# A strided convolution with its gradients on one Trainium2 core: branch A of the first batch split one level further, and the second batch's output gradient turned inside its gelu stage

## The chip, the core and the metric

The program runs on one core of one Trainium2 chip. The metric is the device time of one execution, in microseconds (us); the kernel before took 1272.7 us, the median of 3 runs (1272.4 to 1275.49). The core has a matrix engine (TensorE, PE in the profile; its weight loads are PEld), a vector engine (VectorE, DVE), a scalar engine (ScalarE, ACT), GpSimd (POOL) and SyncE (SP). Each works through its own list of instructions in order and waits for the others by semaphores. Transfers between DRAM and the on-chip memory (SBUF) are issued here mostly from SP, the transposing ones always, and from POOL; 16 DMA engines carry them out. The accumulators of TensorE (PSUM) are eight banks, used here as four tiles of two banks each.

## The reference, cut to what matters

```python
B, T, D, K = 2, 16000, 256, 31      # x is (B, T, D), w is (K, D, D), bf16
s = 2
L = (T - K) // s + 1                # 7985
h = sum over i < K of x[:, i:i + s*L:s, :] @ w[i]      # strided convolution
mu  = sum over l of h / L;  var = sum over l of (h - mu)**2 / L     # per batch and channel
y = gelu((h - mu) / sqrt(var + 1e-5) * gn_gamma + gn_beta)          # tanh form
returns y and, for a given grad_out, the gradients for x, w, gn_gamma, gn_beta
```

The heavy parts are three convolutions of one size: the forward one, the one that gives the gradient of x, and the one that gives the gradient of w.

## The kernel before

**Stages.** In order of time: the forward convolution of batch 0 (four chunks of 512 column pairs, `c` = 0 to 3), the forward convolution of batch 1 with the gelu of batch 0 (its value, its slope and the gradient through it) beside it, the gradient of x for batch 0 with the gelu of batch 1 beside it, the gradient of x for batch 1, and the gradient of w. TensorE's own work never stops for a stage of the others: gelu, normalization and turning of layouts are put beside matmuls on DVE, ACT, POOL and the DMA queues.

**The branches.** The convolution is computed by a splitting of the taps into three products in place of four, applied at two levels. At the first level the taps fall into the branches A, B_ and C_; the inputs of a branch are sums of neighbouring input parts (`sums`) and its weights are parts or differences of the weights (`w_diff`, `w_mid`). Inside each branch the same is done again: its leaves A (`mk_la`) and C_ (`mk_lc`) and its middle product, whose inputs are `mk_ux` and whose weights are `W[br][:, B_]`. The middle product is always computed at a third level (`l3_first` with the weights `WX`, then `l3_rest`). A branch in `self.deep` has its two leaves split a third time as well: `mk_deep` makes two more sums on DVE (tiles `lh` and half of `l`), the leaf needs `rest`, 32 matmuls, and 16 more of a shared product (`third` with the weights `WD`), instead of 64 matmuls. All have 128 x 128 weights and 256 columns (230 or 231 in parts of the last chunk).

In the kernel before `self.deep` holds C_ alone in chunk 0 of batch 0, B_ and C_ in chunks 1 to 3, and nothing in batch 1.

**The order of a chunk.** `fwd_chunk_fixed` writes out the steps in `STEPS`: F (first part of the middle product), L0 and L1 (the leaves), R (rest of the middle product). Two steps, L0 and L1 of "prev", finish branch C_ of the chunk before. `RING` gives each branch two of the four PSUM tiles, `px` and `pt`: the middle product is made in `px`, copied with changed signs to `pt` (`l3_neg`, `seed`, or an ACT copy), and the leaves are accumulated onto it. After each step the functions listed by the number of the step put DVE's work for the steps to come into its list. All this is fixed in program order, so that an instruction that waits holds up everything behind it on its engine.

**The clock of the plan.** Side work is placed by a clock that is counted up with every step (`side_work`, which is `advance`) by an assumed duration, 1.75 for an F step, 3.5 for R, 7.0 for an L step (times .75 where the branch is split). `at(t, fn)` emits `fn` at the first step that ends at or after t. `PLAN` holds such times: loads and parts of the second set of weights (`w2`), turning of the output gradient (`got`, `late`), the gelus (`g0`, `g1`), the elementwise gradient (`e`).

**The second set of weights.** The gradient of x needs the weights with rows and columns turned. `w2_load` turns them with four DMA transposes into a tile `vr` (one buffer, tag "in"), `w2_comp` takes two differences into a tile `vd` on DVE and stores six pieces to DRAM (`vl`), from where they are loaded after the forward stage.

**The output gradient.** The gelu needs grad_out with channels on the partitions. `got_turn` makes that by one DMA transpose for each of eight units (`gt` tiles). For batch 0 this is done in its gelu stage and `grad` works on the `gt` tile. For batch 1 it is done early, beside the forward stage of batch 0: `got_store` writes it to DRAM (`got_d`), and `gelu_load` fetches it again (`gg` tiles) in the gelu of batch 1.

Where the profile names L125, the instruction went through the small recording class `Engine`; L160, L162 and L170 are `w_mid` and `w_deep`. The groups are told apart by the names of tiles: `la`, `lc`, `lh` are leaf inputs, `lx` is `ux`, `s` the sums, `wx` and `wd` the third-level weights, `hs` the evacuated result, `junk` the squares for the statistics, `rb` branch B_'s results.

## Time and profile before

| what | value |
|---|---|
| median of 3 runs | 1272.7 us (1272.4 to 1275.49) |
| the profiled execution | 1270.96 us, of which the span from first to last instruction is 1269.1 us |
| granted TensorE clock, mean | 0.999 |
| busy share of PE, DVE, ACT, POOL | 97%, 71%, 40%, 22% |
| matmuls | 7692 |
| DMA traffic | 252.73 MB, mean 199 GB/s |
| HBM read and written | 136.42 MB, 68.63 MB |

The profile was taken on one execution, which was 1.7 us faster than the median of the others. A page of the profile gives busy time by engine, the span in 40 slices, the DMA queues, the chain of work that ended last, and the costliest groups of instructions. Beside it the trace can be asked for the instructions of a stretch in order of time (start, duration, engine, operation, tiles, and in brackets the idle time before it with what ended it), for groups by shape, for waits, and for the busy time of each engine in given stretches. Durations of merged matmuls include the end of the last one's pipeline; the distance from one start to the next is what a group takes of TensorE's time.

### The profile page before, as it was taken

To read this page: it belongs to the slowest core of one execution; us is meant where nothing else is said; L and a number is where in the kernel's file an instruction comes from. 1 tells how busy PE (TensorE), PEld (TensorE's weight loads), DVE (VectorE), ACT (ScalarE), POOL (GpSimd) and SP (SyncE) were. 2 spreads that over 40 slices of the span, in tenths; PEclk is the share of its full clock that TensorE was granted. 3 is DMA by queue.
4 is the path that set the end of the run, shared out by engine and by line. 5 is a ranking of instruction groups with operands and counts; after the bars stand their busy time and mean duration, and the time that the engine had idled before them with its cause. 6 is when DMAs were issued, how large, how long until landed. Compare 5 with 4: busy or idle time off the path is not lost.

```text
span 1269.1 us, 19006 instructions
## 1 busy us (share of the span) xinstructions
PE 1233.0 (97%) x7692; PEld 758.6 (60%) x7692; DVE 901.7 (71%) x1080; ACT 504.0 (40%) x679; POOL 279.8 (22%) x410
## 2 busy tenths in 40 slices
PE   4899999999999999999999999999999999999998
PEld 2788889988888964444445444445444444444444
DVE  3967656578988687989876596685576755876482
ACT  0032423489888568989853333222011010101000
POOL 2013201112222433445333331100000000110043
PEclk9999999999999999999999999999999999999999
DMA  9979987439997796998649995455894795997895
GB/s 199 176 153 196 215 150 138 79 77 197 185 164 159 208 305 157 208 226 234 172 148 107 241 237 121 127 183 170 277 325 150 232 333 188 322 337 262 252 226 127
DMA packets 289335, 252.73 MB, mean 199 GB/s; under 512 B 197128, under 2 KB 260616, under 8 KB 284128
## 3 DMA queue, kind: packets, MB, share of 16 engines
q1 hardware_dynamic: 254448, 152.60, 50.7%
q0 software_dynamic: 30576, 96.82, 29.7%
q10 hardware_dynamic: 4224, 2.10, 0.8%
q8 instruction: 60, 0.98, 0.3%
q14 instruction: 27, 0.22, 0.1%
HBM read 136.42 MB, written 68.63 MB: 162 GB/s over the span
## 4 chain that ended last, share of the span: by engine, by line
PE 49%; DVE 3%; issue 2%; DMA 1%; ACT 1%; POOL 1%; POOLq 0%; DVEq 0%; ACTq 0%
PE wps L125 28%; PE ps L125 20%; DVE D L125 1%; DMA dyd<-gg 1%; DMA x<-in_x_dram 1%; DVE ps L125 0%; DVE et L125 0%; DVE le L125 0%; DVE go L125 0%; DVE ux L125 0%; POOL he L125 0%; DVE s L125 0%; DMA gg<-got 0%; DVE vk L125 0%; ACT gy L125 0%
## 5 line engine op out<-in xcount | busy, mean ns | idle before, releaser
L125 PEld LDWEIGHTS <-w 128*128 128x128 bf16 x3360 | 327.5, 98 | 57.7 <-issue 10.5
L125 PE MATMUL ps<-v,le 128*128 128x512 bf16 (+3 forms) x1152 | 259.2, 375 | 2.6 <-DVE ps L125 2.4
L125 PEld LDWEIGHTS <-le 128*128 128x128 bf16 (+1 forms) x1280 | 129.9, 102 | 144.8 <-issue 4.3
L125 PEld LDWEIGHTS <-x 128*128 128x128 bf16 x1248 | 122.0, 98 | 144.6 <-DVE x L125 0.6
L125 PE MATMUL ps<-la,w 128*128 128x256 bf16 (+2 forms) x1200 | 135.2, 273 | 18.0 <-DVE la L125 17.7
L125 PE MATMUL wps<-dl,x 128*128 128x512 bf16 (+1 forms) x704 | 150.8, 374 | 0.0
L125 ACT ACTIVATE ps<-ps 128x1024 f32<-128x1024 f32 (+3 forms) x115 | 85.2, 741 | 147.0 <-PE ps L125 147.0
L125 PE MATMUL ps<-lc,w 128*128 128x256 bf16 (+2 forms) x1168 | 129.2, 270 | 0.0
L125 ACT COPY p<-wps 128x1024 f32<-128x1024 f32 x28 | 28.4, 1013 | 211.2 <-PE wps L125 106.7
L125 DVE TENSOR_TENSOR go<-ps,rg 128x1024 bf16<-128x1024 f32 (+1 forms) x64 | 78.0, 1220 | 43.8 <-PE ps L125 29.1
L125 POOL DMA_DIRECT2D out_dram<-we x31 | 22.5, 726 | 334.6 <-DVE we L125 334.6
L125 PE MATMUL ps<-v,ux 128*128 128x512 bf16 (+1 forms) x384 | 90.7, 379 | 3.6 <-DVE ux L125 1.9
L125 PE MATMUL wps<-dl,xe 128*128 128x512 bf16 x416 | 91.7, 379 | 0.0
L125 PE MATMUL ps<-lx,w 128*128 128x256 bf16 (+2 forms) x768 | 86.9, 270 | 1.8 <-ACT ps L125 1.3
L125 ACT ACTIVATE gy<-gh,stats 128x1024 bf16<-128x1024 bf16 x64 | 76.6, 1228 | 7.3 <-DMA gh<-hd 7.3
L125 PE MATMUL wps<-D,x 128*128 128x512 bf16 x352 | 77.1, 379 | 0.0
L125 PEld LDWEIGHTS <-xe 128*128 128x128 bf16 x416 | 40.7, 98 | 49.1
L125 PEld LDWEIGHTS <-ux 128*128 128x128 bf16 (+1 forms) x384 | 38.7, 101 | 49.3 <-DVE ux L125 3.6
L125 ACT ACTIVATE hs<-ps 128x512 bf16<-128x512 f32 (+1 forms) x64 | 36.7, 578 | 75.9 <-PE ps L125 75.9
L125 DVE TENSOR_TENSOR ps<-ps,rb 128x1024 f32<-128x1024 f32 (+1 forms) x37 | 38.0, 1028 | 36.2 <-ACT rb L125 28.3
L125 ACT COPY rg<-ps 128x1024 f32<-128x1024 f32 (+1 forms) x32 | 32.2, 1007 | 69.2 <-PE ps L125 67.4
L125 DVE SCALAR_TENSOR_TENSOR gz<-gy,gy 128x1024 bf16<-128x1024 bf16 x32 | 39.1, 1222 | 23.9 <-ACT gy L125 22.8
(170 smaller groups left out, 1708.4 us busy)
## 6 DMA issues: line engine op xcount, KB each, us to landing
x<-in_x_dram SPq DMA_DIRECT2D x29, 1024.0 KB, 8.6
xe<-in_x_dram SPq DMA_DIRECT2D x20, 1024.0 KB, 9.2
S<-dnd SPq DMA_DIRECT2D x16, 1216.0 KB, 8.3
D<-dnd SPq DMA_DIRECT2D x12, 1216.0 KB, 9.2
out_dram<-go POOLq DMA_DIRECT2D x28, 512.0 KB, 4.2
gh<-hd POOLq DMA_DIRECT2D x32, 256.0 KB, 7.3
dnd<-dn POOLq DMA_DIRECT2D x32, 256.0 KB, 4.4
E<-dnd SPq DMA_DIRECT2D x6, 1216.0 KB, 10.6
```

Of the source, the lines that this page charges most:

```text
L125: ins = fn(*a, **k)
```

## The change

Three things are changed together.

1. In chunks 1 to 3 of batch 0 branch A is split like B_ and C_. Its shared third-level products come in two new steps, V and T, and F accumulates onto V in the same PSUM tile: V (leaf A's product into `px[A]`), an ACT copy of it to SBUF (`l3_keep`), L0 of B_, F, T (leaf C_'s product into `pt[A]`), a DVE sum (`l3_sum`), R, and then two DVE operations that make `pt[A]` (`l3_seed`) in place of an ACT copy. `w_deep(A)` makes the weights. The lists of DVE work by step are rearranged, also for batch 1, and the clock counts a split leaf with half of 7.0 instead of three quarters.
2. The output gradient of batch 1 is turned inside the gelu of batch 1, as for batch 0. The stores to `got_d`, the loads from it and the tiles `gg` are gone.
3. `w2_comp` takes the differences in place in `vr` instead of in `vd`; the stores of the unchanged parts come earlier, in `w2_keep`. Some times of the plan are moved: the `w2` parts, the first elementwise part of the gradient stage, the statistics of batch 1, and the places of `w2x_comp(A)` and of `mk_l(B_)` at the start of the gradient stage. `small` has one buffer instead of two, `wd` six instead of four.

```diff
-            t = WD[br, lf] = side["p"].tile([P, 2, 2, 2, D], BF16, name="wd", tag="wd", bufs=4)
+            t = WD[br, lf] = side["p"].tile([P, 2, 2, 2, D], BF16, name="wd", tag="wd", bufs=6)
...
+    def w2_keep(q, raw):
         sl = slice(q * 512, (q + 1) * 512)
-        for br, r1 in ((A, 0), (C_, 1)):
+        for br, r1 in ((C_, 1), (A, 0)):
             for slot, r2 in ((A, 0), (C_, 1)):
                 gq.dma_start(out=vl_d[br][:, slot // 2, :, sl], in_=raw[:, :, r2, r1, :])
+    def w2_comp(q, raw):
+        sl = slice(q * 512, (q + 1) * 512)
+        for slot, r in ((A, 0), (C_, 1)):
+            ve.tensor_tensor(out=raw[:, :, r, 1, :], in0=raw[:, :, r, 1, :], in1=raw[:, :, r, 0, :], op=ALU.subtract)
+            gq.dma_start(out=vl_d[B_][:, slot // 2, :, sl], in_=raw[:, :, r, 1, :])
...
-            self.deep = () if b else (C_,) if c == 0 else (B_, C_)
+            self.deep = () if b else (C_,) if c == 0 else ORDER
...
+        def l3_leaf(self, br, lf, ps):
+            l = self.l[br, lf]
+            self.third(ps[:, 0], (l[0] if isinstance(l, tuple) else l)[:, 1], WD[br, lf])
+        def l3_keep(self, px):
+            self.v = side["m"].tile([P, 512], FP32, name="vf", tag="jk", bufs=1)
+            ac.copy(out=self.v[:], in_=px[:, 0, :])
+        def l3_sum(self, pt):
+            ve.tensor_tensor(out=self.v[:], in0=pt[:, 0], in1=self.v[:], op=ALU.add)
+        def l3_seed(self, px, pt):
+            ve.tensor_tensor(out=pt[:, 0], in0=self.v[:], in1=px[:, 0], op=ALU.subtract)
+            ve.scalar_tensor_tensor(out=pt[:, 1], in0=px[:, 1], scalar=-1.0, in1=self.v[:], op0=ALU.mult, op1=ALU.subtract)
...
-                at(clock[0] + 2, lambda: self.squares(br))
+                at(clock[0] + 1.5, lambda: self.squares(br))
...
+        if A in k.deep:
+            steps[4:7] = [(4, "V", A, 1.75), (5, "L0", B_, 7.0), (12, "F", A, 1.75), (13, "T", A, 1.75), (6, "R", A, 3.5)]
...
-            side_work(us * (.75 if own and what[0] == "L" else 1))
+            side_work(us * (.5 if own and what[0] == "L" else 1))
...
-            for fn in {0: (lambda: k.sums(A),), 1: (lambda: k.mk_lc(B_),), 2: (lambda: k.mk_la(A),), 3: (lambda: k.mk_ux(A),),
-                       5: (lambda: k.mk_lc(A), lambda: k.sums(C_)), 6: (lambda: k.mk_la(C_),),
+            for lf in {1: (A,), 4: (C_,)}.get(n, ()):
+                if B_ in k.deep:
+                    k.mk_deep(B_, lf)
+            for fn in {0: (lambda: k.sums(A),), 1: (lambda: k.mk_lc(B_), lambda: k.mk_la(A)), 3: (lambda: k.mk_ux(A),),
+                       4: (lambda: k.mk_lc(A),),
+                       5: (lambda: k.sums(C_),), 6: (lambda: k.mk_la(C_),),
...
-            for br, lf in {1: ((B_, A),), 4: ((B_, C_),), 8: ((C_, A),), 9: ((C_, C_),)}.get(n, ()):
+            for br, lf in {6: ((A, A),), 8: ((A, C_),), 9: ((C_, A),)}.get(n, ()):
...
-    def got_store(c, e, gt):
-        for dh in range(2):
-            gq.dma_start(out=got_d[c][e][:, dh], in_=got_view(c, gt, dh))
...
-        go = new("gg", 1)
-        gq.dma_start(out=go[:], in_=got_d[c][e][:, dh])
-        return h[:], go[:]
+        return h[:]
...
         def turn_in(u):
-            if b == 0 and u < 8:
-                gts[u] = got_turn(0, *units[u])
+            if u < 8:
+                gts[u] = got_turn(b, *units[u])
...
-    PLAN = dict(got=(22, 42, 64, 84, 120), late=(2, 11), w2=((3, 16), (29, 43), (52, 66)),
+    PLAN = dict(w2=(6, 14, 48, 82),
...
-                e=((0, 1, None, None, 3, 5.5), (0, 2, 30, 38, 56, 63), (0, 3, 92, 98, 114, 121), (1, 0, 172, 180, 203, 208),
+                e=((0, 1, None, None, 9, 13), (0, 2, 30, 38, 56, 63), (0, 3, 92, 98, 114, 121), (1, 0, 172, 180, 203, 208),
...
+    at(7, lambda: w_deep(A))
...
+    at(PLAN["w2"][0], lambda: w2_comp(0, wr.pop(0)))
+    for q, t in zip((1, 2, 3), PLAN["w2"][1:]):
+        at(t, lambda q=q: wr.__setitem__(q, w2_load(q)))
+        at(t + 13, lambda q=q: w2_keep(q, wr[q]))
+        at(t + 25, lambda q=q: w2_comp(q, wr.pop(q)))
...
-    at(1.8, lambda: fwd_stats(1))
+    at(4.5, lambda: fwd_stats(1))
...
     kn.mk_ux(B_)
-    kn.mk_l(B_)
     kn.sums(A)
     w2x_comp(C_)
+    kn.mk_l(B_)
...
-            marks[0][A, "R"] = [lambda: w2x_comp(A)]
+            marks[0][A, "R"] = marks[0][A, "L0"]
+            marks[0][A, "L0"] = [lambda: w2x_comp(A)]
```

More of the change, by code (lines that the diff above doesn't have):

```diff
@@ L518, in fwd_chunk_fixed @@
                 k.l3_neg(px[br])
+            elif what == "V":
+                k.l3_keep(px[A])
+            elif what == "T":
+                k.l3_sum(pt[A])
+            elif what == "R" and br == A:
+                if deep:
+                    k.l3_seed(px[A], pt[A])
+                else:
+                    ac.activation(out=pt[A][:], in_=px[A][:], func=ACT.Copy, scale=-1.0)
+                ve.tensor_tensor(out=px[A][:], in0=px[A][:], in1=rb[:, 0], op=ALU.add)
             elif what == "R" and (br == C_ or own):
@@ L1454, in conv_stem_kernel @@
     epool = tc.tile_pool(name="ep", bufs=1, side="right", reuse_waits="tile")
-    for i, t in zip((6, 7), PLAN["late"]):
-        parked(i, t)
     done = gelu_plan(0, *PLAN["g0"])
```

65 lines of the change are left out of this document (26 added, 39 removed).

## The prediction

> **What bounds the kernel now.** The page comes first: its busy times say which engine has no room.
>
> ```profile
> PE 1233.0 (97%) x7692; PEld 758.6 (60%) x7692; DVE 901.7 (71%) x1080; ACT 504.0 (40%) x679; POOL 279.8 (22%) x410
> ```
>
> TensorE is busy for 1233.0 of 1269.1 us, but an average over stages does not say where a saved matmul shortens the run. So the second view is the busy time by stretch, for chunks 1, 2 and 3 of batch 0's forward stage and for the start of the gradient stage (columns: stretch, length, busy PE, PEld, DVE, ACT, POOL with counts, granted clock, DMA share, GB/s).
>
> ```profile
> 77.90:129.20 51.30, 51.30 (x466) 45.13 (x465) 38.45 (x50) 17.30 (x33) 12.72 (x17) 1.00 0.85 167
> 129.20:180.50 51.30, 51.30 (x467) 45.10 (x466) 32.23 (x43) 17.30 (x33) 9.93 (x13) 1.00 1.11 206
> 180.50:228.60 48.10, 48.10 (x467) 45.14 (x465) 30.82 (x44) 17.21 (x33) 4.66 (x7) 1.00 0.60 111
> 459.60:480.20 20.60, 17.41 (x79) 7.27 (x78) 18.88 (x33) 17.31 (x24) 3.84 (x6) 1.00 0.83 238
> ```
>
> In the three chunks that the change touches TensorE has no idle time at all, at full clock, while DVE is busy for 30.82 to 38.45 us of some 50. There a removed matmul is removed time, as long as DVE and ACT, in their fixed order, still come before it. The last row is the opposite: 20.60 - 17.41 = 3.2 us of idle TensorE where the gradient stage begins, with DVE at 18.88. The change moves DVE work there too.
>
> **Part 1, the matmuls removed.** The third view is TensorE's list in order of time; a group's cost is the distance to the next start. First an unsplit leaf and a split one of full width:
>
> ```profile
> 106.31 1.92 PE L125 MATMUL ps<-s,wx 128*128 128x256 bf16 x16
> 108.07 7.18 PE L125 MATMUL ps<-la,w 128*128 128x256 bf16 x64
> 115.09 3.71 PE L125 MATMUL ps<-lx,w 128*128 128x256 bf16 x32
> ...
> 154.04 1.94 PE L125 MATMUL ps<-lc,w 128*128 128x256 bf16 x16
> ...
> 157.60 1.92 PE L125 MATMUL ps<-s,wx 128*128 128x256 bf16 x16
> ...
> 169.93 1.94 PE L125 MATMUL ps<-la,wd 128*128 128x256 bf16 x16
> 171.70 1.94 PE L125 MATMUL ps<-lc,wd 128*128 128x256 bf16 x16
> ```
>
> Branch A's leaf takes 115.09 - 108.07 = 7.02 us. A split leaf takes 157.60 - 154.04 = 3.56 us for its 32 matmuls, and its shared product 171.70 - 169.93 = 1.77 us. Split, a leaf is 7.02 - 3.56 - 1.77 = 1.69 us shorter; chunks 1 and 2 have four such leaves: 6.76 us. In chunk 3 only the 230 or 231 wide parts shrink:
>
> ```profile
> 204.20 1.75 PE L125 MATMUL ps<-lc,w 128*128 128x231 bf16 x16
> ...
> 207.37 1.92 PE L125 MATMUL ps<-s,wx 128*128 128x256 bf16 x16
> 209.13 6.51 PE L125 MATMUL ps<-la,w 128*128 128x231 bf16 x64
> 215.48 3.34 PE L125 MATMUL ps<-lx,w 128*128 128x231 bf16 x32
> 218.66 1.94 PE L125 MATMUL ps<-la,wd 128*128 128x256 bf16 x16
> 220.44 1.94 PE L125 MATMUL ps<-lc,wd 128*128 128x256 bf16 x16
> ```
>
> (215.48 - 209.13) - (207.37 - 204.20) - (220.44 - 218.66) = 6.35 - 3.17 - 1.78 = 1.40 us, twice 2.80. Together **9.56 us** less of TensorE, with 96 fewer matmuls (32 a chunk).
>
> **Part 2, what the split asks of DVE and ACT.** Their rows, by shape, over the three chunks (mean ns):
>
> ```profile
> L125 DVE TENSOR_TENSOR ps<-ps,rb 128x1024 f32<-128x1024 f32 x9 | 11.1, 1230 | 7.9 <-ACT ps L125 4.7 <-ACT rb L125 3.2
> L125 DVE TENSOR_TENSOR ps<-ps,rb 128x512 f32<-128x512 f32 x12 | 8.4, 700 | 23.1 <-ACT rb L125 22.9
> L125 DVE TENSOR_TENSOR la<-s,s 128x2064 bf16<-128x2064 bf16 x6 | 7.4, 1225 | 0.0
> L125 DVE TENSOR_TENSOR lh<-la 128x1028 bf16<-128x1028 bf16 x6 | 4.2, 697 | 5.3 <-PE ps L125 5.3
> L125 ACT ACTIVATE hs<-ps 128x512 bf16<-128x512 f32 x22 | 12.9, 593 | 40.4 <-PE ps L125 40.4
> L125 ACT ACTIVATE junk<-hs 128x1024 bf16<-128x1024 bf16 x12 | 12.6, 1053 | 0.2
> L125 ACT ACTIVATE ps<-ps 128x512 f32<-128x512 f32 x9 | 5.2, 582 | 5.7 <-PE ps L125 5.7
> ```
>
> Each chunk gains four leaf sums of 0.70, one `l3_sum` and two `l3_seed` operations of 0.70 on DVE: 4.9 us, on 38.45 at most, in a chunk that shrinks to 51.3 - 3.4 = 47.9 us. That is 90%, so it is a question of order, not of load. With the starts of TensorE's groups laid out anew from F of branch B_ (0 us), R of A ends at 28.35, L1 of B_ at 31.9, F of C_ at 33.7, and L0 of A follows. Between R and L0, 3.56 + 1.76 = 5.32 us, DVE must do the two seeds, the 128x1024 addition to `px[A]`, `mk_la(C_)` and both halves of `mk_deep(A, A)`: 1.40 + 1.23 + 1.23 + 1.40 = 5.26 by the rows. This is the tightest place: about 0.1 us late in chunks 1 and 2, and in chunk 3, where L1 is 3.17, the window is 4.93 and the list 0.3 to 0.4 late. I charge **+0.5 us**; the bounds are 0 (successive starts lie up to 0.1 apart less than the durations) and 3 (0.2 us of handing over on each of five operations, in three chunks).
>
> The ACT copy between V and F has cover: after L1 of "prev" ACT does two evacuations, two squares and the copy, 1.2 + 2.1 + 0.6 = 3.9 us, while TensorE does V and L0 of B_, 1.77 + 3.56 = 5.3 us. Without these 1.4 us F would wait. Branch C_'s seeds now have L1 of A (3.56) and F (1.76) to hide in instead of 7.02 + 1.76: the ACT copy after the leaves (1.0) and two additions (1.4) end 2.4 us after the leaves, 2.9 us in time. `w_deep(A)` (two operations of 1.2 us) stands where DVE waited for ACT's `rb` before (22.9 us in that row) and costs nothing.
>
> **Part 3, the second weights in place.** DVE's subtraction now overwrites data whose stores must have landed, and the next load must wait for the stores of the difference. Rows for the loads, the wait for them, and the landing of the stores (KB each, median us from issue):
>
> ```profile
> 96.72 14.09 SPq L125 DMA_TRANSPOSE vr<-in_w_dram  x4
> ...
> 115.99 0.69 DVE L125 TENSOR_TENSOR vd<-vr 128x1024 bf16<-128x1024 bf16 x1 [1.59 <-DMA vr<-in_w_dram]
> ...
> vl<-vr POOLq DMA_DIRECT2D x16, 256.0 KB, 6.2
> ```
>
> The four loads of one part took up to 115.99 - 96.72 = 19 us. In the new order part 1 can be loaded from some 18 us into chunk 1 (the difference of part 0 at 11.6, then its stores), is there at 30 to 37, and its stores land 7 us later, at 37 to 44; DVE comes to the subtraction at 40, just ahead of branch C_'s seeds, which have 2.5 us to spare. Part 2 is loaded from about 1 us into chunk 2, stored by 20 to 27, and wanted at 25.6, where DVE would idle until R of A ends at 28.35. Part 3 has more room. So each waits between nothing and 1.5 us beyond its cover; I take **+0.6 us** in sum, with bounds 0 and 3. The load on the DMA engines falls here, which is why I take the lower half: seven of the eight units of grad_out and their stores leave these chunks.
>
> **Part 4, grad_out turned in the gelu.** What a turned byte costs the DMA engines is read from two stretches: 129.2 to 180.5, where q1 carries only transposes, and 893 to 1139, where it carries plain loads (columns: packets, MB, share of 16 engines); the third row is POOL's queue from 480.2 to 660, the last the median us to landing of a unit of grad_out in the first stretch.
>
> ```profile
> q1 hardware_dynamic: 24635, 6.20, 80.2%
> ...
> q1 hardware_dynamic: 45232, 65.41, 79.3%
> ...
> q0 software_dynamic: 9735, 31.88, 64.6%
> ...
> gt<-in_grad_out_dram SPq DMA_TRANSPOSE x4, 7.2
> ```
>
> Transposes: 0.802 x 51.3 / 6.20 = 6.6 us of all engines for a MB; plain loads 0.793 x 246 / 65.41 = 3.0; POOL's transfers 0.646 x 179.8 / 31.88 = 3.6. Eight turned units of 0.52 MB take 27 us of the gelu stage's 180 and sixteen `gg` loads of 0.26 MB give 15 back: the mean share there rises by 12 / 180 = 0.07. [...]
>
> It adds no time, because each unit is asked for two halves of the gelu (22 us) before `grad` needs it and lands in 7.2. SP's list takes eight more instructions among the dn transposes, which are only stored for a later stage; POOL's loses 32. DVE's and ACT's operations keep their shapes. I charge **0**, bounds -0.5 and +1.
>
> **Part 5, the start of the gradient stage.** TensorE's idle there is in these waits:
>
> ```profile
> 459.62 1.02 PE L125 MATMUL ps<-vx,et 128*128 128x512 bf16 x4
> ...
> 461.53 1.89 PE L125 MATMUL ps<-v,ux 128*128 128x512 bf16 x8 [0.89 <-ACT ps L125]
> ...
> 468.78 1.89 PE L125 MATMUL ps<-v,ux 128*128 128x512 bf16 x8 [0.48 <-ACT ps L125]
> ...
> 475.21 1.04 PE L125 MATMUL ps<-vx,s 128*128 128x512 bf16 x4 [1.10 <-DVE vx L125]
> ...
> 480.18 1.90 PE L125 MATMUL ps<-v,ux 128*128 128x512 bf16 x8 [0.48 <-DVE ux L125]
> ```
>
> `w2x_comp(A)` moves ahead of the elementwise part and of `mk_l(C_)`, 2.8 us of DVE, and the second sign copy ahead of ACT's square root; that takes away most of 1.10 + 0.48 + 0.48. Against it, batch 0's last gelu halves are emitted later: the clock now counts 3.5 us less in front of them, so their last product stands behind R of A of the last chunk instead of before it, and with it the elementwise part that ends in `vx`, the first weights of the stage.
>
> ```profile
> 444.62 0.76 DVE L125 TENSOR_SCALAR et<-et,stats 128x2080 bf16<-128x2080 bf16 x1 [5.29 <-DMA et<-dyd]
> ...
> 455.68 1.22 DVE L125 TENSOR_TENSOR vx<-v 128x2048 bf16<-128x2048 bf16 x1
> ```
>
> By the order of the lists that product now has the addition and `mk_la(C_)` ahead of it, 2.46 us by part 2's rows; its store and the loads `et` follow. I take 1.8, since they took DVE's time before, too. `vx` was done 459.62 - 456.90 = 2.7 us ahead of its use, so the delay shows only in the waits of `vx` for C_ and of `le`, some 1 us in all. Net **-1.0 us**, bounds -2.2 (all three waits gone, no delay) and +3.5 (the 3.5 us of clock in full, nothing gained). The 177 us of batch 1's forward stage have slack of one leaf step at each hand-over; the shuffle of DVE's list there is put at **+0.4**, bounds 0 and +2.
>
> **The sum.** -9.56 + 0.5 + 0.6 + 0 - 1.0 + 0.4 = -9.1 us on the profiled execution of 1270.96: 1261.9. That execution was 1.7 us below the median of the runs shown, so the median to expect is 1272.7 - 9.1 = **1263.6 us**.
>
> **Rivals.** They are priced from the forecast. A wait of TensorE can cost more than itself: after one of 2.33 us 16 matmuls took 3.01 us, where the row at 106.31 has 1.92, so 1.1 us more.
>
> ```profile
> 53.36 3.01 PE L125 MATMUL ps<-s,wx 128*128 128x256 bf16 x16 [2.33 <-DVE wx L162]
> ```
>
> [...]
>
> - *The list between R and L0 sets the pace.* If each chunk loses 1 to 1.5 us there and the weights' waits come to 2 us, the gain halves: 1263.6 + 2.5 to 3.5 + 1.4 = about 1268. For it speaks the 5.26 us in a window of 5.32; against it DVE's successive starts, which lie closer than its durations.
> - *The gelu ends too late for the gradient stage.* Part 5 comes out at +3.5 instead of -1.0: 1268.1. For it speaks that the elementwise part already waited 5.29 us for its load; against it the 2.7 us between `vx` and its use.
> - *More is gained.* All waits of part 5 go and the emptier DMA queues keep DVE from waiting at all: 1272.7 - 9.56 - 2.2 = 1260.9.
> - *Slower than before.* The in-place subtraction of part 2 in chunk 2 holds DVE. With loads of 19 us and stores of 10 us (an estimate, above the row's 6.2) part 1's stores land at 18 + 19 + 1 + 10 = 48 us instead of by 42.5: 5.5 lost. Its difference is stored at 60, 12 us into chunk 2; part 2's stores land there at 12 + 19 + 1 + 10 = 42, where the cover ends at 28.35: 13.6 lost. With twice 1.1 that is 21 us: 1285. It decides from 9.1 us lost in these two places. What speaks against it is a DMA share that falls in these chunks.
>
> **How the numbers follow.** The forecast (1260.5 to 1266) has 0.60, the two rivals near 1268 together 0.22, the greater gain 0.07, the slower one 0.06, and 0.05 is left for a result near no change by several of these together. A measurement of this kernel can tell 0.3%, 3.8 us, from no change. Faster by more (below 1268.9): all of the first and third, most of the second: 0.87; within 0.3%: 0.07; slower: 0.06. The range 1259.5 to 1268.5 takes in the bounds of parts 2 to 5 that do not all fall together.
>
> **What would show it.** Right: 7596 matmuls; chunks 1 and 2 at 47.9 to 48.5 us and chunk 3 near 45.5, with waits of TensorE under 0.5 us before L0 of A; no `vr` wait of DVE over 2.5 us; less than 2.5 us of idle in the first 20 us of the gradient stage; a DMA share higher by 0.05 to 0.1 in the gelu of batch 1. Wrong: a wait of 1 us or more in each chunk before L0 of A (first rival), `et` loads for which TensorE stands idle (second), DVE held by `vl` stores (the last).

## The result and the profile after

The changed kernel took 1265.77 us, the median of 5 runs (1263.28 to 1268.05), beside 1273.06 us (1272.4 to 1275.49, 5 runs) for the kernel before: a ratio of 0.9939, 95% interval 0.992 to 0.9959. It is faster by 7.3 us. The forecast was 1263.6 us in a range of 1259.5 to 1268.5. The profiled execution took 1264.1 us, its span 1262.3 us (before: 1270.96 and 1269.1).

The page's busy times of after (share of the span and instructions of each engine):

```profile
PE 1223.9 (97%) x7596; PEld 749.3 (59%) x7596; DVE 916.5 (73%) x1103; ACT 502.6 (40%) x679; POOL 259.3 (21%) x378
```

7596 matmuls are the 96 fewer that were named. POOL has 32 instructions less, DVE 23 more. The busy times of after by stretch: chunks 1, 2 and 3 of batch 0, then the forward stage of batch 1, the first 81 us of the gradient stage, and the rest; behind it the same last three stretches of before (columns as in the prediction: stretch, length, busy PE, PEld, DVE, ACT, POOL, granted clock, DMA share, GB/s).

```profile
76.60:124.70 48.10, 48.10 (x435) 42.08 (x433) 40.26 (x53) 16.75 (x33) 8.55 (x11) 1.00 0.64 118
124.70:172.75 48.05, 48.05 (x435) 42.02 (x433) 36.70 (x50) 16.75 (x33) 9.54 (x13) 1.00 0.88 167
172.75:218.55 45.80, 45.42 (x434) 41.97 (x432) 36.73 (x52) 16.66 (x33) 3.23 (x4) 1.00 0.81 138
...
218.55:450.32 231.77, 230.11 (x2146) 208.15 (x2144) 184.71 (x271) 172.58 (x255) 63.10 (x89) 1.00 0.77 158
450.32:531.25 80.93, 73.94 (x342) 32.91 (x340) 70.15 (x109) 68.68 (x80) 27.22 (x40) 1.00 0.91 201
531.25:1262.30 731.05, 722.95 (x3376) 337.42 (x3376) 502.01 (x524) 204.85 (x236) 138.05 (x200) 1.00 0.76 218
```

```profile
228.56:459.62 231.06, 230.30 (x2147) 208.06 (x2146) 182.39 (x269) 172.46 (x255) 65.20 (x92) 1.00 0.79 166
459.62:537.88 78.26, 73.67 (x342) 33.01 (x340) 68.47 (x105) 68.89 (x80) 28.86 (x44) 1.00 0.88 207
537.88:1269.10 731.22, 723.10 (x3376) 337.31 (x3376) 502.15 (x524) 204.54 (x236) 142.92 (x208) 1.00 0.78 217
```

By the starts of the chunks' first matmuls (76.59, 124.67, 172.74, 218.55 against 77.93, 129.21, 180.5, 228.56 before) and these rows the spans differ as follows. Terms that fell are negative.

| stretch | before | after | difference | forecast |
|---|---|---|---|---|
| up to chunk 1 | 77.93 | 76.59 | -1.34 | 0 |
| chunks 1 to 3 | 150.63 | 141.96 | -8.67 | -9.56 + 0.5 + 0.6 = -8.46 |
| forward stage of batch 1 | 231.06 | 231.77 | +0.71 | +0.4 |
| first 81 us of the gradient stage | 78.26 | 80.93 | +2.67 | -1.0 |
| the rest | 731.22 | 731.05 | -0.17 | 0 |
| sum | 1269.1 | 1262.3 | -6.8 | -9.1 |

So the chunks gave in sum what was forecast, and the start of the gradient stage, where a gain of 1 us was expected, took 2.67 us back. The waits of TensorE that make this up, in order of time:

```profile
205.47 1.75 PE L124 MATMUL ps<-la,w 128*128 128x231 bf16 x16 [0.38 <-DVE la L124]
...
279.50 3.71 PE L124 MATMUL ps<-lx,w 128*128 128x256 bf16 x32 [1.66 <-DVE gy L124]
...
452.24 1.89 PE L124 MATMUL ps<-v,ux 128*128 128x512 bf16 x8 [0.89 <-ACT ps L124]
454.90 1.02 PE L124 MATMUL ps<-vx,s 128*128 128x512 bf16 x4 [0.78 <-DVE vx L124]
466.02 1.04 PE L124 MATMUL ps<-vx,s 128*128 128x512 bf16 x4 [1.36 <-DVE vx L124]
471.48 1.90 PE L124 MATMUL ps<-v,ux 128*128 128x512 bf16 x8 [0.96 <-DVE ux L124]
477.02 1.02 PE L124 MATMUL ps<-vx,et 128*128 128x512 bf16 x4 [0.61 <-DVE go L124]
478.98 3.61 PE L124 MATMUL ps<-v,le 128*128 128x512 bf16 x16 [0.94 <-ACT ps L124]
482.89 1.89 PE L124 MATMUL ps<-v,ux 128*128 128x512 bf16 x8 [0.30 <-ACT ps L124]
```

From 452 to 483 these are 5.84 us. In the same part of before there were 3.13 us in five waits (0.89, 0.18, 0.48, 1.10, 0.48), of which the moves were meant to clear the last three. The 0.38 in chunk 3 is also what its stretch lacks of busy time, 45.80 - 45.42.

### The profile page after: what moved, and what is told of

The parts are those of the page before. It is cut to its first block, busy times and chain, and to the rows that moved or that the text cites. A ratio compares the mean times of both kernels' runs of the same rounds, so it can differ in the third digit from the quotient of the medians.

```text
span 1262.3 us, 18788 instructions
## 1 busy us (share of the span) xinstructions
PE 1223.9 (97%) x7596; PEld 749.3 (59%) x7596; DVE 916.5 (73%) x1103; ACT 502.6 (40%) x679; POOL 259.3 (21%) x378
## 4 chain that ended last, share of the span: by engine, by line
PE 75%; issue 7%; DVE 6%; DMA 6%; ACT 3%; SPq 1%; POOL 1%; POOLq 0%; DVEq 0%; ACTq 0%
PE ps L124 46%; PE wps L124 29%; DMA hd<-hs 1%; DMA gh<-hd 1%; SPq L124 1%; DVE ps L124 1%; DMA xt<-in_x_dram 1%; DMA dn<-et 1%; DMA dyd<-gt 1%; DVE et L124 1%; DVE gz L124 1%; DMA dnd<-dn 1%; DVE gy L124 1%; DVE s L124 1%; ACT gs L124 0%
## 5 line engine op out<-in xcount | busy, mean ns | idle before, releaser
L124 PEld LDWEIGHTS <-w 128*128 128x128 bf16 x3168 | 309.0, 98 | 56.4 <-issue 11.2
L124 ACT ACTIVATE ps<-ps 128x512 f32<-128x512 f32 (+2 forms) x112 | 82.1, 733 | 136.4 <-PE ps L124 131.8
L124 PE MATMUL ps<-la,w 128*128 128x256 bf16 (+2 forms) x1056 | 120.0, 273 | 16.7 <-DVE la L124 16.7
L124 PE MATMUL ps<-lc,w 128*128 128x256 bf16 (+2 forms) x1024 | 113.9, 270 | 0.0
L124 POOL DMA_DIRECT2D out_dram<-go x32 | 23.3, 728 | 167.2 <-DVE go L124 156.0
```

Source lines behind the costliest of these rows:

```text
L124: ins = fn(*a, **k)
```

## The experiments

All start from the changed kernel. A profile gives one execution, and executions of one kernel differ by some microseconds (after's five runs by 4.8, before's by 3.1), so each run is read by its stretches first and by its median second. The ratios are to the kernel before on the same chip. The runs are spread over several chips, on which the kernel before has medians from 1268.33 to 1273.06 us, so medians of different chips can't be set side by side. By the ratios no version is told apart from the changed kernel as faster.

| run | chunks 1 to 3 | batch 1's forward | first part of the gradient stage | median, us | ratio to before (95%) |
|---|---|---|---|---|---|
| before | 150.63 | 231.06 | 78.26 | 1273.06 | |
| after | 141.96 | 231.77 | 80.93 | 1265.77 | 0.9939 (0.992 to 0.9959) |
| after, again | 141.97 | 231.23 | 80.55 | 1266.11 | 0.9949 (0.9928 to 0.997) |
| A unsplit | 150.64 | 231.40 | 81.21 | 1275.27 | 1.0028 (1.0003 to 1.0052) |
| gelu of batch 0 early | 141.96 | 233.38 | 79.64 | 1269.06 | 0.9975 (0.9941 to 1.0009) |
| old order at the start | 141.96 | 234.17 | 79.20 | 1269.51 | 0.9983 (0.9959 to 1.0007) |
| plain loads for turned units | 141.96 | 231.72 | 82.23 | 1267.84 | 0.9966 (0.9947 to 0.9984) |
| two of four moves undone | 141.96 | 230.69 | 79.34 | 1262.62 | 0.9954 (0.994 to 0.9969) |
| squares later | 141.97 | 230.39 | 80.22 | 1262.68 | 0.9958 (0.9941 to 0.9974) |
| leaf's sum first | 141.09 | 230.58 | 80.66 | 1261.8 | 0.9953 (0.9935 to 0.9971) |
| first turn later | 141.96 | 230.97 | 80.30 | 1263.06 | 0.9949 (0.9919 to 0.9978) |
| joined | 141.09 | 230.70 | 78.67 | 1265.8 | 0.9941 (0.9921 to 0.9962) |
| joined, gelu of batch 1 later | 141.09 | 230.21 | 77.07 | 1271.38 | 0.9984 (0.9961 to 1.0008) |
| joined, `he` first | 141.09 | 230.17 | 78.67 | 1260.13 | 0.9943 (0.9924 to 0.9962) |

**Is it the split alone?**

```diff
-            self.deep = () if b else (C_,) if c == 0 else ORDER
+            self.deep = () if b else (C_,) if c == 0 else (B_, C_)
...
-    at(7, lambda: w_deep(A))
```

> The changed kernel with branch A's leaves unsplit again in chunks 1 to 3 of batch 0 (everything else of the change stays). First theory: the split alone makes the 8.7 us that the three chunks became shorter, and the rest of the change gives nothing: chunks at 51.3, 51.3 and 48.1 us, 7692 matmuls, median 1265.8 + 8.7 = 1274.5 us, about the time of the kernel before or 1 us above it. Rival: the emptier transfer queues of these chunks (no grad_out units parked there) gave a part of it: chunks under 51.0 us and a median of 1272 us or less.

The three chunks of this run by stretch:

```profile
77.28:128.57 51.29, 51.29 (x466) 45.14 (x464) 37.08 (x49) 17.06 (x33) 9.59 (x13) 1.00 0.70 128
128.57:179.86 51.29, 51.29 (x467) 45.11 (x465) 32.20 (x43) 17.06 (x33) 8.45 (x12) 1.00 0.85 170
179.86:227.92 48.06, 48.06 (x467) 45.09 (x464) 32.01 (x45) 16.98 (x33) 3.23 (x4) 1.00 0.57 102
```

150.64 us, as before to a hundredth, although the DMA share is 0.70, 0.85 and 0.57 where before had 0.85, 1.11 and 0.60. The transfers that left these chunks gave nothing there; the split gave all of it. The median is not below that of the kernel before (ratio 1.0003 to 1.0052), so no gain of the rest of the change together is seen.

**The list between R and L0 of A.**

```diff
+            if n == 6 and A in k.deep:
+                k.mk_deep(A, A)
...
-            for br, lf in {6: ((A, A),), 8: ((A, C_),), 9: ((C_, A),)}.get(n, ()):
+            for br, lf in {8: ((A, C_),), 9: ((C_, A),)}.get(n, ()):
```

> The changed kernel with the split sum of branch A's first leaf put ahead of the sum `la` of branch C_ on DVE. The prediction's part 2 has the list between R and L0 of A 0.1 us late in chunks 1 and 2 and 0.3 to 0.4 in chunk 3, which the trace of after bears out (0.38 in chunk 3): without the 1.23 us of `la` of C_ in it, L0 starts at once, the chunks take 47.9, 47.9 and 45.4 us, 0.7 us less in sum. Rival: `la` of C_ is then late for the next product and the chunks stay at 48.1, 48.1 and 45.8 or grow.

DVE's list in order of time at this place of chunk 1, in after:

```profile
105.24 0.69 DVE L124 TENSOR_TENSOR ps<-vf,ps 128x512 f32<-128x512 f32 x1 [2.85 <-PE ps L124]
105.97 0.70 DVE L124 SCALAR_TENSOR_TENSOR ps<-ps,vf 128x512 f32<-128x512 f32 x1
106.70 1.23 DVE L124 TENSOR_TENSOR ps<-ps,rb 128x1024 f32<-128x1024 f32 x1
107.84 1.22 DVE L124 TENSOR_TENSOR la<-s,s 128x2064 bf16<-128x2064 bf16 x1
108.98 0.69 DVE L124 TENSOR_TENSOR lh<-la 128x1028 bf16<-128x1028 bf16 x1
109.71 0.70 DVE L124 TENSOR_TENSOR la<-la 128x1032 bf16<-128x1032 bf16 x1
```

The six operations run from 105.24 to 110.41 without a gap, the first of them 0.26 us after TensorE went on to L1 of B_ (104.98), and L0 began at 110.46, 0.16 us after TensorE could have. In chunk 3 the same 5.48 us lie between the start of L1 of B_ (199.99) and L0 of A (205.47), but L1 and F take only 4.94 us there, so L0 is 0.54 us late; the trace's 0.38 is less by 0.16, because a group's duration includes the end of its pipeline: 1.92 us for this F, while the group behind such an F can start 1.76 us after it (106.31 and 108.07 in before). With `la` of C_ behind the leaf's sum the chunks take 47.91, 47.91 and 45.27 us, 141.09 in sum. The list cost 141.96 - 141.09 = 0.87 us, near the 0.16, 0.16 and 0.54 read from the starts in the three chunks. And 150.63 - 141.09 = 9.54 us is what the removed matmuls are worth without any stall; the prediction had 9.56.

**The wait in batch 1's forward stage.** The profile puts the 1.66 us at 279.50 down to `gy` on DVE. ACT's list in after before that time:

```profile
273.50 1.15 ACT L124 ACTIVATE gy<-gy,kb 128x1024 bf16<-128x1024 bf16 x1 [3.32 <-DVE gz L124]
...
276.64 1.05 ACT L124 ACTIVATE junk<-hs 128x1024 bf16<-128x1024 bf16 x1
...
277.81 1.06 ACT L124 ACTIVATE junk<-hs 128x1024 bf16<-128x1024 bf16 x1
...
278.87 0.58 ACT L124 ACTIVATE ps<-ps 128x512 f32<-128x512 f32 x1
```

The sign copy of branch B_ (`ps<-ps`) ends at 279.45, 0.05 us before TensorE goes on, and stands behind two squares (`junk`). The change had moved the squares from 2 to 1.5 on the planner's clock, which is less than an F step's 1.75, so they come ahead of the copy.

```diff
-                at(clock[0] + 1.5, lambda: self.squares(br))
+                at(clock[0] + (2 if self.b else 1.5), lambda: self.squares(br))
```

> The changed kernel with the squares of batch 1's chunks 0.5 us later on the planner's clock (2 instead of 1.5, as in the kernel before); in batch 0 they stay. First theory: the wait of 1.66 us at 279.50 (1.60, 1.28 and 2.40 in other runs) is for ACT's sign copy of branch B_, which stands behind two squares of 1.06 us; with the squares behind it the wait falls under 0.3 us and batch 1's forward stage is 1.3 us or more shorter than 231.8 us. Rival: it is DVE's `gy` operation, as the profile names it, or ACT's earlier wait for `gz`: then 1 us or more of it stays.

There the copy was done at 276.86 and TensorE did not wait; batch 1's forward stage took 230.39 us, 1.38 less than in after. The first theory holds: the releaser that the profile names was not the cause. How long the wait is varies: in other runs with the squares in front it was 1.28, 2.40, 1.60, 0.57, 0.47, 0.86 and 1.11 us, and nothing in the next run, where batch 0's gelu comes earlier and ACT's wait for `gz` ahead of the squares is 1.29 us instead of 3.32. So it seems to take both: the squares ahead of the copy, and an ACT that the gelu has already held up (the 3.32 us in the first row above).

**The start of the gradient stage: the clock of the plan.**

```diff
-                g0=(33.0, 10.6), g1=(18.0, 11.2),
+                g0=(29.5, 10.6), g1=(18.0, 11.2),
...
-    at(19.3, lambda: fwd_stats(0))
+    at(15.8, lambda: fwd_stats(0))
```

(The load of B_'s second weights moves from 212 to 208.5 with them.)

> The changed kernel with batch 0's gelu planned 3.5 us earlier, which takes back the 3.5 us that the planner's clock now counts less in batch 1's forward stage. First theory: those 3.5 us are what made the elementwise part and with it `vx` late at the start of the gradient stage: the last `gt` product comes about 4 us earlier against that start, `vx` of branch B_ is ready over 2 us ahead of its use, the wait of 0.78 us for `vx` of C_ falls to 0.2, and the median is 0.6 to 2.3 us lower (1263.5 to 1265.2). Rival: the waits of that start hang on the load of the third second weights (`v` of A) and on the store of `hs`, which do not move: the waits of 1.36 and 0.96 us stay and the median moves by under 0.6 us. The wait of 1.66 us in batch 1's forward stage: gone if batch 0's gelu operations cause it, there if the squares in front of the sign copy do.

Rows of DVE's list in before, in after and in this run: batch 0's last gelu product and B_'s `vx` (that of before, 455.68, is in the prediction).

```profile
424.90 0.69 DVE L125 TENSOR_TENSOR gt<-gy,gt 128x1024 bf16<-128x1024 bf16 x1
```

```profile
419.23 0.68 DVE L124 TENSOR_TENSOR gt<-gy,gt 128x1024 bf16<-128x1024 bf16 x1
...
448.26 1.22 DVE L124 TENSOR_TENSOR vx<-v 128x2048 bf16<-128x2048 bf16 x1
```

```profile
417.23 0.68 DVE L124 TENSOR_TENSOR gt<-gy,gt 128x1024 bf16<-128x1024 bf16 x1
...
447.46 1.22 DVE L124 TENSOR_TENSOR vx<-v 128x2048 bf16<-128x2048 bf16 x1
```

Against the first matmul of the gradient stage (459.62, 450.32 and 452.10) the product stands at -34.7, -31.1 and -34.9, and the end of B_'s `vx` at -2.7, -0.8 and -3.4. So the 3.5 us of the clock did arrive as 3.6, but cost only the 0.60 us by which the wait for C_'s `vx` grew (0.18 to 0.78); here it is gone. A's `vx` was waited for no less than in after (1.50 us, there 1.36), as the rival had it, and the 0.61 and 0.94 stayed; the wait of 0.96 for `ux`, which the rival also kept, was gone. The median did not fall: the earlier gelu met new waits in batch 1's forward stage (233.38 us).

**The start of the gradient stage: the moves.**

```diff
-                e=((0, 1, None, None, 9, 13), (0, 2, 30, 38, 56, 63), (0, 3, 92, 98, 114, 121), (1, 0, 172, 180, 203, 208),
+                e=((0, 1, None, None, 3, 5.5), (0, 2, 30, 38, 56, 63), (0, 3, 92, 98, 114, 121), (1, 0, 172, 180, 203, 208),
-    at(4.5, lambda: fwd_stats(1))
+    at(1.8, lambda: fwd_stats(1))
+    kn.mk_l(B_)
-    kn.mk_l(B_)
-            marks[0][A, "R"] = marks[0][A, "L0"]
-            marks[0][A, "L0"] = [lambda: w2x_comp(A)]
+            marks[0][A, "R"] = [lambda: w2x_comp(A)]
```

> The changed kernel with the order of the kernel before at the start of the gradient stage (the first elementwise part at 3 and 5.5, the statistics at 1.8, `mk_l(B_)` ahead of `w2x_comp(C_)`, `w2x_comp(A)` after the elementwise part). The prediction's step: the moves take away 2 us of waits, so without them the median is 1 to 2 us higher (1266.8 to 1267.8) and the waits of 0.48 us each come back. Rival, from the trace of after: the moves only hand the waits on, since `v` of A lands late anyway and DVE's `et` additions now stand ahead of `go`: the sum of TensorE's waits in the first 35 us of the stage stays within 0.7 us of 5.9, and the median within 0.7 us of 1265.8.

The first part of the stage was 79.20 us instead of 80.93: the 0.96, 0.61, 0.94 and 0.30 are gone, the 1.36 for A's `vx` is 0.26, and 2.05 stands for the 0.78. The 2.05 has two parts: `mk_l(B_)` is in front of C_'s `vx` again, and B_'s `vx` ends 0.8 us ahead of the stage as in after; in before, with the same order but 2.7 us ahead, the wait was 0.18. Both expectations missed: in the profiled executions the moves cost 1.7 us in this stretch. The median points the other way (0.9983), on a chip where this kernel's runs spread over 13 us. In the profiled run batch 1's forward stage, with the same instructions, was 2.40 us longer, nearly all of it at the squares' wait: 2.40 us instead of 1.66, and 5.35 instead of 3.71 us for the matmuls behind it. What the moves are worth in the whole is not settled by it. The second run undoes only the first line and the statistics:

> The changed kernel with two of the four moves at the start of the gradient stage undone: the first elementwise part at 3 and 5.5 and the statistics at 1.8 again; `w2x_comp` of C_ and A stay early. First theory, from the run with all four undone (79.2 us from the first `vx,et` to the wait of 531, where the changed kernel takes 80.9): the late elementwise part is what costs, since its `et` operations and `gz`, which waits for the store of `hs`, stand ahead of `ux` and `go`; then the waits for `ux` (0.96) and `go` (0.61) go and the wait for `vx` of C_ stays at 0.8: 78.5 to 79.5 us. Rival: the early `w2x_comp` is what costs, by the `le` and `s` behind it; then the stage's first 80 us stay at 80.5 or more.

79.34 us, within the first theory's range, but not with the waits it gave: those for `go`, for the sign copy after it and the 0.30 went, that for `ux` stayed (1.23), and one of 1.88 us for a sign copy came. ACT's list there:

```profile
459.63 0.30 ACT L124 ACTIVATE stdv<-var,eps_t 128x2 f32<-128x2 f32 x1 [3.89 <-DVE var L124]
459.83 0.58 ACT L124 ACTIVATE ps<-ps 128x512 f32<-128x512 f32 x1
```

The square root waits 3.89 us for DVE and the sign copy waits behind it. So early statistics bring a wait of 1.88 us, and the late elementwise part brings the other three, 1.85 us in sum. What the later statistics earn is less than 1.88: A's `vx`, which TensorE waits for in after (1.36), is not waited for here. Why the elementwise part costs is in after's rows, first DVE's, then ACT's:

```profile
469.86 1.22 DVE L124 SCALAR_TENSOR_TENSOR gz<-gy,gy 128x1024 bf16<-128x1024 bf16 x1 [1.94 <-DMA hd<-hs]
...
474.59 1.24 DVE L124 TENSOR_TENSOR et<-et,he 128x2080 bf16<-128x2080 bf16 x1 [2.16 <-ACT he L124]
475.75 1.22 DVE L124 TENSOR_TENSOR go<-ps,rg 128x1024 bf16<-128x1024 f32 x1
```

```profile
471.12 1.15 ACT L124 ACTIVATE gy<-gy,kb 128x1024 bf16<-128x1024 bf16 x1 [3.38 <-DVE gz L124]
472.17 2.38 ACT L124 ACTIVATE he<-he,stats 128x1040 bf16<-128x1040 bf16 x2
```

`gz` waits for the stores of `hs`. Behind it on DVE stands `ux`; behind the ACT operation that waits for `gz` stands `he`, behind that DVE's `et` addition, and behind that `go`, for which TensorE waits. In before the `et` additions stood ahead of `gz`, and its wait for the stores was 0.98 us instead of 1.94.

**The turned units.**

```diff
+        if b:
+            for dh in range(2):
+                gq.dma_start(out=gt[:, :, dh, off:off + MH], in_=h_d[b][:, dh, :, e, 2 + c * MH:2 + (c + 1) * MH])
+            return gt
```

> The changed kernel with batch 1's gelu reading another tensor of the same size by two plain loads on POOL's queue where it turned grad_out (the values of grad_out of batch 1 are left out). First theory (the prediction's part 4): the turning is hidden, the median stays within 1 us of 1265.8, and only the share of the transfer engines in the gelu of batch 1 falls, by 0.05 or so. Rival: the turned units slow the transfers at the start of the gradient stage (the first took 13.2 us while `v` of A and `hs` were under way): without them `v` of A lands before DVE wants it, the waits of 1.36 and 0.96 us shrink to under 0.5 each, and the median is 1.5 to 3 us lower.

The other run asks for the first unit later:

```diff
-            turn_in(0)
+            if b:
+                at(now[0] + 6, lambda: turn_in(0))
+            else:
+                turn_in(0)
```

> The changed kernel with the first unit of batch 1's grad_out turned 6 us later, behind the load of `v` of A instead of beside it. First theory: that turn slows the load of `v` of A (its wait was 1.36 us with the turn and 0.51 with plain loads in its place): the wait for `vx` of A falls to 0.5 us and the first 80 us of the gradient stage take 0.5 to 1 us less than 80.9. Rival: the load is slow for the stores of `hs` and the loads of `gh`, which stay: no change by over 0.3 us.

With plain loads the wait for A's `vx` was 0.51 us, but that for `ux` 3.11, and the stretch was no shorter (82.23). The share of the transfer engines in the gelu was 0.81, and the ratio to before (0.9966) is no lower than after's, so no gain from leaving the turns out is seen. With the first turn later the wait for A's `vx` was 0.51 us too, and the stretch took 80.30. But that wait was also 0.51 in two runs that left the turn in its place (squares later, and the changed kernel again), and 2.95 in a third (leaf's sum first). The load of A's `v` is issued as the last forward leaf frees its buffer (at 450.51 in after), and DVE got it 11.9 us later in after and 13.5 us later with the leaf's sum first, so its landing differs that much with the turn in place. Whether the turn slows it stays open.

**The joined versions.** The first run repeats the changed kernel; joined is squares later, leaf's sum first and the elementwise part at 3 and 5.5; joined with batch 1's gelu later has `g1=(20.5, 11.2)` besides.

> The changed kernel once more, for the comparison with the two joined versions on one chip, and for what repeats between executions. First theory: chunks at 48.08, 48.07 and 45.81 us again to 0.05, since no wait for a transfer lies there; the waits for `ux` (1 us), `go` (0.61) and the sign copy (0.94) at the start of the gradient stage again; the waits for the sign copy in batch 1 (0.5 to 2.4 us so far) and for `vx` of A (0.5 to 2.9) differ, since loads stand behind them. Rival: the extra waits of that start were chance, and the first 80 us take 79 or less.

> The changed kernel with three edits: squares of batch 1 later, the first leaf's split sum ahead of `la` of C_, and the first elementwise part of the gradient stage back at 3 and 5.5, the statistics staying at 4.5. First theory: they add up: chunks 141.1 us in sum, no wait over 0.3 us for batch 1's sign copy, no wait for `go`, none of 1.88 us for the sign copy behind the square root; first 80 us of the gradient stage at 78.5 to 79.5, and the median 3 us or more below that of the changed kernel on the same chip. Rival: a gain ahead only makes the loads of `v` and the store of `hs` late: the waits for `vx` of A and `ux` grow by what was gained, and the median is within 1.5 us of the changed kernel's.

> The joined version with batch 1's gelu planned 2.5 us later (20.5 instead of 18). First theory: `gz`, which waits until the stores of `hs` have landed, then stands behind `ux` on DVE, so that the wait of about 1 us of TensorE for `ux` goes: first 80 us of the gradient stage 0.7 to 1.2 us shorter than in the joined version. Rival: gelu's operations then stand in front of other parts of the stage and the wait turns up elsewhere: no change or longer.

The repeat bears out what repeats: chunks of 48.08, 48.07 and 45.82 us, waits of 0.62 and 0.93 for `go` and the sign copy, and 80.55 us for the start. The wait for `ux` does not repeat so closely (1.46 us). Joined made its gains over after, 0.9 in the chunks, 1.1 in batch 1's forward stage and 2.3 at the start, and gave them back at one place, not the one that the rival named (`vx` of A 1.85, `ux` 0.57 us). TensorE's row there, POOL's list and ACT's list around it:

```profile
574.39 6.49 PE L124 MATMUL ps<-v,le 128*128 128x512 bf16 x16 [3.96 <-ACT ps L124]
```

```profile
563.15 1.52 POOL L124 DMA_DIRECT2D dnd<-dn  x2 [6.63 <-DMA dn<-et]
...
565.21 3.82 POOL L124 DMA_DIRECT2D he<-hd  x6
```

```profile
572.26 1.17 ACT L124 ACTIVATE he<-he,stats 128x944 bf16<-128x944 bf16 x1 [8.31 <-DMA he<-hd]
```

POOL waits for a turned `dn` to store it; the `he` loads are behind; ACT waits 8.31 us for them, and its sign copy comes right after, at 573.34. The wait and the slower matmuls after it (6.49 us, against 3.61 for the same group at 478.98 in after) make 6.8 us. The run with two moves undone had the same chain: 10.85 us on POOL, 7.04 on ACT, 2.69 on TensorE. In before nothing stood between the `dn` turns on SP's list; now the units of grad_out do. The `dn` turn behind such a unit started at 561.97 in joined, 563.24 with two moves undone and 559.21 in after, and POOL's store began 1.1 to 1.2 us later each time. No run takes the units out of joined, and with plain loads in their place the changed kernel's store still waited 1.98 us, so how much of the wait the units make is not shown. Before's row and after's:

```profile
569.22 1.52 POOL L125 DMA_DIRECT2D dnd<-dn  x2
```

```profile
560.45 1.53 POOL L124 DMA_DIRECT2D dnd<-dn  x2 [4.49 <-DMA dn<-et]
```

The version with the gelu later met its expectation at the start (77.07 us), and its profiled execution took 1258.5 us, less than any other profiled one. But its other runs took 1268.3 us or more, and no profile shows them: where they lose is open.

**The loads `he` ahead of the stores.** Joined, and in it

```diff
-                e=((0, 1, None, None, 3, 5.5), (0, 2, 30, 38, 56, 63), (0, 3, 92, 98, 114, 121), (1, 0, 172, 180, 203, 208),
+                e=((0, 1, None, None, 3, 5.5), (0, 2, 30, 38, 56, 63), (0, 3, 92, 94, 114, 121), (1, 0, 172, 180, 203, 208),
```

> The joined version with the loads `he` of batch 0's last part planned at 94 instead of 98, so that they stand in front of the stores `dnd` on POOL's list. In the joined run these stores waited 6.6 us for the turned `dn`, which stand behind the turned grad_out on SP's list; the `he` loads behind them were issued at 565.2, ACT waited 8.3 us for them with its sign copy behind, and TensorE 3.96 us at 574.39, with 6.49 instead of 3.61 us for the 16 matmuls after it. First theory: that is why the joined version's median was only 0.3 us below the changed kernel's; with the loads in front the wait at 574 is under 0.5 us, and the median is 5 to 7 us below the joined version's 1265.8, that is 1259 to 1261, or 0.990 to 0.991 of the kernel before. Rival: the loads themselves are slow while SP's turns run; then ACT still waits over 3 us for `he`, and the median stays within 2 us of 1265.8.

ACT no longer waits for `he` there, and the largest wait of TensorE near 574 is one of 0.61 us at 583.86. From 526.96 to 746.19 this run takes 219.23 us where joined has 225.48 for the same work:

```profile
526.96:746.19 219.23, 217.00 (x1016) 103.27 (x1017) 173.02 (x267) 134.28 (x154) 85.22 (x129) 1.00 0.84 197
```

```profile
527.08:752.56 225.48, 219.89 (x1017) 103.92 (x1017) 173.22 (x267) 134.24 (x154) 89.94 (x136) 0.98 0.85 196
```

That the wait for `he` makes these 6.25 us is shown. The median, 1260.13 us, lies in the range expected, but the ratio does not (0.9943, on a chip where the kernel before took 1268.33): two of its eight runs took 1264.4 and 1267.2. Its profiled span, 1258.7 us, is 3.6 below after's; by the ratios it is not told apart from the changed kernel.

## Why the prediction was right, and where it was not

The median came 2.2 us above the forecast, inside the range. By the stretches of the profiled execution the mechanism that carries the sum, the removed matmuls, is right. That the total came so near is in part luck: 1.34 us of the 6.8 lie where nothing was forecast, two errors in the chunks (+0.37 and -0.6) partly cancel, and the start of the gradient stage went the other way.

- **The matmuls removed (-9.56): right.** 9.54 us where nothing waits. It came from groups of the same form in the trace of before.
- **The list between R and L0 (+0.5): right in place, too small.** 0.87 us: 0.16 in chunks 1 and 2, where 0.1 was said, 0.54 in chunk 3, where 0.3 to 0.4 was. The operations themselves took 5.17 us, even less than the 5.26 of the sum; what it left out is the 0.26 us ahead of the first. No run shows the 0.2 us of handing over on each operation that its upper bound was made from: the six ran without a gap. The first rival, 1 to 1.5 us a chunk, fell.
- **The second weights in place (+0.6): 0.** DVE's four pairs of `vr` operations waited for no transfer, the loads and stores being done before the slots. Even the lower half of the range was too much; the rival that ended slower hung on this and fell. The premise holds in part: the share of the transfer engines fell to 0.64 and 0.88 in chunks 1 and 2, but rose in chunk 3, from 0.60 to 0.81, and the stores of six units of grad_out left these chunks, not of seven.
- **grad_out turned in the gelu (0): right in the profiled run, wrong in its reason.** The DMA share in batch 1's gelu was 0.05 higher than in before, and 0.03 higher in the repeat of the same kernel (rows below), where the prediction worked out 0.07 from its 6.6 and 3.6 us for a MB; with the first turn later it was 0.81, as in before. So one execution's share does not size the rise. By queue, SP's transposes took 26.2% of the engines for 7.81 MB in after's stretch, 6.0 us of all engines for a MB, and POOL's plain transfers 59.1% for 28.21 MB, 3.8 us; in the repeat these were 6.1 and 3.6. By these figures a turned MB took the engines 1.6 and 1.7 times as long here as one of POOL's plain transfers. What the prediction passed over are the eight turns' places on SP's list, because the `dn` turns behind them "are only stored for a later stage". The stores of `dn` stand on POOL's list ahead of `he`, on which ACT's sign copies hang. After's profiled run had room for it; two others did not. The stretch of the gelu in before, then in after and in the repeated run (the same window), where the last but one figure is the share:

```profile
480.20:660.00 179.80, 178.07 (x838) 82.10 (x839) 152.11 (x225) 149.32 (x169) 81.38 (x124) 1.00 0.81 201
```

```profile
470.90:650.70 179.80, 175.90 (x826) 80.78 (x827) 155.43 (x229) 153.04 (x172) 75.47 (x115) 1.00 0.86 201
...
470.90:650.70 179.80, 176.16 (x827) 80.93 (x828) 155.16 (x228) 152.94 (x172) 75.55 (x115) 1.00 0.84 201
```

- **The start of the gradient stage (-1.0): this step failed.** It came to +2.67, inside its bounds of -2.2 and +3.5. Of the three waits to be cleared one went (0.48 for ACT). That for A's `vx` (1.10) stayed, at 1.36: DVE waited 0.80 us at 462.41 for `v` to land, which no order of its list changes, and in four runs where TensorE's wait was 0.51 that is what the list alone left. That for `ux` grew from 0.48 to 0.96, behind `gz`. TensorE was idle for 3.4 us of the stage's first 20.6 (3.2 in before), where under 2.5 was named as a sign of being right. The late `vx` cost 0.60, near the "some 1 us" given. The term that was missing is 1.85 us: the waits of 0.61, 0.94 and 0.30 behind the later elementwise part, which the prediction did not follow through the list. The second rival, in which the last gelu ends too late for this stage, covers only the 0.60; the third, in which more is gained, needed all the waits gone and fell with this step.
- **Batch 1's forward stage (+0.4): +0.71, near by luck.** The 0.4 was put down for DVE's list. What cost was ACT's: a new wait of 1.66 us from the squares ahead of the sign copy, less smaller ones that went (0.43 and 0.33). With the squares back the stage took 230.39 us, 0.67 less than in before.
- **The 1.34 us ahead of chunk 1 were not in the sum.** They lie in the first load: TensorE waited 16.31 us for its first `la`, 17.66 in before, ahead of every changed instruction. In the twelve other profiled executions it waited 15.98 to 17.56 us, so most of it looks like chance; with one execution of before that is not shown. Without them the profiled gain is 5.5 us, where 9.1 was forecast.

## What to carry to other kernels

Here the removed matmuls, in a stretch with no idle time, could be priced to 0.02 us from groups of the same form (9.56 forecast, 9.54 measured); the uncertainty sat where lists were reordered (-1.0 forecast, +2.67 measured). There, follow each moved operation through everything that stands behind it on its engine, and through the engine behind that, and ask of each wait to be cleared whether it ends on an order or on a transfer: DVE's 0.80 us here were for `v` to land, and the order of DVE's own list does not bring that forward. A plan's clock that is recalibrated moves every timed item against the untimed ones, so an item half a microsecond to the other side of a step can stand ahead of the copy that TensorE needs (the squares here: 0.5 on the clock, 1.66 us of TensorE's wait).

## What the runs showed of the chip

In the profiled executions a wait of TensorE of 2.05 us or more was mostly followed by slower matmuls, one of 1.88 us or less, the start of the program apart, by none in the rows read. The rows, from the run with two moves undone, from the one with the old order (two), and from the one with the leaf's sum first:

```profile
460.46 1.89 PE L124 MATMUL ps<-v,ux 128*128 128x512 bf16 x8 [1.88 <-ACT ps L124]
```

```profile
280.08 5.35 PE L124 MATMUL ps<-lx,w 128*128 128x256 bf16 x32 [2.40 <-DVE gy L124]
...
458.40 1.44 PE L124 MATMUL ps<-vx,s 128*128 128x512 bf16 x4 [2.05 <-DVE vx L124]
```

```profile
465.61 1.89 PE L124 MATMUL ps<-vx,s 128*128 128x512 bf16 x4 [2.95 <-DVE vx L124]
```

After 1.88 us eight matmuls took their usual 1.89; after 2.05, 2.40 and 2.95 us the groups took 1.44, 5.35 and 1.89 where the same groups elsewhere take 1.02, 3.71 and 1.02. In these rows the granted clock goes with it: it is 1.00 from 460.46 to 462.20, behind the 1.88 us, and 0.65 (458.40 to 460.00), 0.67 (280.08 to 285.20) and 0.50 (465.61 to 467.40) behind the others. So in these rows the loss sets in between a wait of 1.88 us and one of 2.05. It is no firm bound: in three of the fourteen profiled executions, the repeated one among them but not before's, the sixteen matmuls after the wait of 2.33 us took their usual time (1.93 or 1.94 us; 2.78 to 3.55 in the other eleven), at a granted clock of 1.00 where before had 0.62 (53.36 to 56.20):

```profile
53.83 1.93 PE L124 MATMUL ps<-s,wx 128*128 128x256 bf16 x16 [2.33 <-DVE wx L161]
```
